# S4D convolution and SwiGLU on one core: skip term on TensorE, kernel stage in 64 by 64 pairs, loads in small paced pieces, and a new deal of the tasks

## The chip, the cores and the metric

The kernel runs on one core of one Trainium2 chip. The metric is device time in microseconds (us) of one execution. Three executions of the kernel before took 968.3, 971.08 and 966.05 us; the median is 968.3 us. The execution that the profiler recorded took 967.95 us, of which 966.0 us lie between its first and last instruction (the span).

## The reference, cut to what matters

The input u is 2048 tokens of 640 channels in float32. A six-fold modulation (shift, scale and gate, twice) comes from a small vector c through silu and one matrix. Then:

```
h = layernorm(x) * (1 + ca) + sa
K[d, l] = 2 Re sum_n C[d, n] exp(A[d, n] dt[d] l)          # 128 states, 2048 taps
y = irfft(rfft(h, 4096) * rfft(K, 4096))[:2048] + h * D_skip
x = x + ga * y
h = layernorm(x) * (1 + cb) + sb
x = x + gb * ((silu(h @ w1) * (h @ w3)) @ w2)              # 640 -> 1728 -> 640
```

The skip term h * D_skip is the same as adding D_skip[d] to the tap at lag 0 of the kernel K, and that is how both kernels make it.

## The kernel before, in words

**First stage (0 to about 350 us): the convolution.** The 640 channels are dealt in 5 blocks of 128 (b = 0 to 4). For each block the kernel K is generated in 8 chunks of 16 channels: GpSimd makes integer phases (`ph`) and products (`yy`, `xx`), ScalarE makes sines (`tr`), VectorE multiplies them on, and TensorE sums over the states into a bank `kps` (32 matmuls of 64 columns, on four tiles of 32 columns). ScalarE copies `kps` into `ks`, and VectorE adds D_skip to the one column in 64 that holds the tap at lag 0 (`skip`, L1342). A Fourier transform in two factors follows, by matmuls: the first factor turns `ks` (and the normalized input `xb`) into a bank `ps` (8 tasks for each block and each of the two, 8 matmuls of 128 columns in each task, L1400), which ScalarE or VectorE copy to `sp`; the second turns `sp` into the spectra `fh` (input) and `fk` (kernel). VectorE multiplies the spectra (`product`, `both`, L1446 and L1454, into `fp`), TensorE turns them back by one factor (`fz`), ScalarE or VectorE copy that to `zt`, and a DMA stores `zt` to the scratch `zd` in HBM.

**The tail (about 336 to 398 us).** When the last chunk of the last block is generated, its buffers are freed (`change`, L1113) and the second stage's buffers open in their place: the first 512 tokens (`low`), the matrix `wd` of the last transform, the first two tiles of the weights (`wr_0`, `wr_13`, `w2r`), and rows of `zd` for `iy`. `iy` (L551) is the last factor: it gives the convolution's output for the tokens, which VectorE adds to them. The 512 channels of the blocks 0 to 3 go first (two halves u = 0, 1), then the last 128 channels, read back when the last `zt` is stored ("the read-back"; its matmuls are L562). Between them stand 8 matmuls `awake`, whose result nobody reads. A layer norm of the tokens and four transposes of them follow.

**Second stage (398 us to the end): the feed-forward network.** Four token blocks of 512; the first two go through 14 tiles of the 1728 columns (`f-tiles`, in the order 0, 13, 1, 2, ...; tile 13 has 64 columns), each as three matmul products of a high and a low half of both operands (`gu`, L999 to L1001), then gate, split and `down` (`acc`, L1036). The last two blocks go together through `pair_up` and `pair_down`. Weights are loaded by `weights_load` (L667) one or two tiles ahead, split by ScalarE (`wh`, L693) and VectorE or GpSimd (`wl`).

**What sets the order.** In the first stage and the tail every engine's instructions stand in the order in which a table of task numbers, ORDER, deals the tasks (class Plan, L162; a letter behind a number picks the engine where a task can go to two). The class InOrder (L138) makes each engine keep that order; while its field `behind` is set, what is issued also waits for the last TensorE instruction that was issued before it. `held_back` (L1733) makes a DMA wait for the read-back's last matmul, once `hold` is set. SyncE's queue (SP) issues nearly all DMAs, in its own order; a DMA at its front that waits keeps those behind it.

## Time and profile before

| quantity | value |
|---|---|
| median of three executions | 968.3 us |
| profiled execution, its span | 967.95 us, 966.0 us |
| mean granted TensorE clock | 0.964 |
| TensorE matmuls busy | 856.0 us (89%) |
| VectorE busy | 713.6 us (74%) |
| ScalarE busy | 518.4 us (54%) |
| GpSimd busy | 336.2 us (35%) |
| moved by DMA | 113.20 MB, mean 117 GB/s |

A line of the groups reads: source line (L147 stands for all that goes through InOrder), engine, operation, output<-inputs, shape, count | busy us in all, mean ns of one | idle time of the engine ahead of them and what ended it. A line of the windows reads: stretch in us, its length, then for PE (matmuls), PEld (weight loads), DVE (VectorE), ACT (ScalarE) and POOL (GpSimd) the busy us and the number of instructions, then the granted clock, the busy share of the DMA engines and GB/s. A float32 matmul leaves two records, so 32 matmuls read x64.

### The profile page before, as it was taken

The numbers are of one execution on the slowest core, as the hardware profiler recorded it, in microseconds if no ns is written. First come the engines' busy times: TensorE is split into PE (matmuls) and PEld (weight loads), VectorE is DVE, ScalarE is ACT, GpSimd is POOL, SyncE is SP. The second block draws the span as 40 slices with busy tenths as digits, with TensorE's granted clock in tenths as the row PEclk, the third lists the DMA queues.
The fourth block names the chain that finished last, engine by engine and source line by source line (L and its number), as shares of the span: only waits on it lengthen the run. The fifth ranks groups of instructions, "written<-read, shape, count | busy, mean of one in ns | idle before, by whom it ended". The sixth has DMA issues, their size and how long they took to land.

```text
span 966.0 us, 20403 instructions
## 1 busy us (share of the span) xinstructions
PE 856.0 (89%) x8145; PEld 681.2 (71%) x8145; DVE 713.6 (74%) x1292; ACT 518.4 (54%) x874; POOL 336.2 (35%) x345
## 2 busy tenths in 40 slices
PE   2164867899999996899999999999999999999997
PEld 1033755787878772577787778888888888888875
DVE  7888899999999974565666486566468777765763
ACT  5889879979888840442343244344234444445331
POOL 2799898599999730100000000000113222300000
PEclk9597889999999997999999999999999999999999
DMA  9955426624040277875545263233031111123242
GB/s 245 253 172 209 106 61 168 162 70 111 25 111 25 69 224 230 200 202 150 158 121 137 82 157 103 82 85 106 28 82 55 55 55 55 42 82 92 86 150 82
DMA packets 124934, 113.20 MB, mean 117 GB/s; under 512 B 12328, under 2 KB 107048, under 8 KB 123432
## 3 DMA queue, kind: packets, MB, share of 16 engines
q1 hardware_dynamic: 124072, 110.99, 42.4%
q8 instruction: 64, 1.05, 0.5%
q10 hardware_dynamic: 768, 0.92, 0.4%
q14 instruction: 30, 0.25, 0.1%
HBM read 90.91 MB, written 20.97 MB: 116 GB/s over the span
## 4 chain that ended last, share of the span: by engine, by line
PE 57%; DVE 2%; DMA 2%; ACT 1%; issue 0%; SPq 0%; DVEq 0%; ACTq 0%
PE p L789 17%; PE acc L1036 16%; PE gu L999 7%; PE gu L1001 6%; PE gu L1000 6%; DMA wq<-in_w 1%; PE iy L562 1%; PE awake L147 1%; PE q L789 1%; PE tp L613 1%; PE fz L147 1%; DMA zd<-zt 0%; PE acc L147 0%; DVE w2l L988 0%; PE iy L147 0%; DVE wq L983 0%
## 5 line engine op out<-in xcount | busy, mean ns | idle before, releaser
L999 PE MATMUL gu<-xh,wh 128*128 128x512 f32 x270 | 106.0, 398 | 0.9 <-ACT xh L581 0.7
L1001 PE MATMUL gu<-xh,wl 128*128 128x512 f32 x270 | 105.4, 390 | 0.0
L1000 PE MATMUL gu<-xl,wh 128*128 128x512 f32 x270 | 105.2, 390 | 0.0
L789 PE MATMUL p<-x,wch 128*128 128x512 f32 x312 | 92.6, 390 | 0.0
L808 POOL TENSOR_TENSOR ws<-wp 128x256 f32<-128x256 f32 x13 | 9.6, 740 | 230.9 <-DVE x L582 116.0
L147 POOL TENSOR_TENSOR yy<-e,e 128x512 f32<-128x512 f32 x80 | 86.0, 1089 | 4.8 <-PE kps L147 3.6
L147 POOL TENSOR_TENSOR ph<-p,p 128x1024 int32<-128x1024 int32 x40 | 78.0, 1953 | 16.4 <-ACT tr L147 16.0
L147 DVE TENSOR_TENSOR yy<-yy,tr 128x512 f32<-128x512 f32 (+1 forms) x80 | 75.3, 946 | 1.6 <-POOL yy L147 1.2
L147 PE MATMUL kps<-yy,xx 128*32 128x64 f32 x2560 | 51.3, 235 | 23.2 <-DVE xx L147 12.9
L693 ACT ACTIVATE wh<-wr 128x640 fp32r<-128x640 f32 x51 | 34.9, 731 | 68.2 <-PE gu L1000 61.1
L147 PEld LDWEIGHTS kps<-yy,xx 128*32 128x32 f32 x2560 | 45.0, 117 | 34.0 <-issue 16.2
L789 PEld LDWEIGHTS p<-x,wch 128*128 128x128 f32 x312 | 58.3, 188 | 12.5 <-ACT s L824 0.4
L999 PEld LDWEIGHTS gu<-xh,wh 128*128 128x128 f32 x270 | 50.6, 188 | 16.8 <-issue 2.1
L1001 PEld LDWEIGHTS gu<-xh,wl 128*128 128x128 f32 x270 | 50.7, 188 | 11.3 <-DVE wl L702 0.4
L1000 PEld LDWEIGHTS gu<-xl,wh 128*128 128x128 f32 x270 | 50.7, 188 | 10.2 <-DVE xl L582 0.2
L789 PE MATMUL p<-x,wcl 128*128 128x512 f32 x156 | 57.0, 389 | 0.0
L147 ACT ACTIVATE tr<-ph,hpi 128x512 f32<-128x512 f32 x80 | 54.5, 689 | 3.0 <-DVE yy L147 2.1
L147 DVE TENSOR_TENSOR xx<-tr,xx 128x512 f32<-128x512 f32 x80 | 54.4, 682 | 1.7 <-ACT tr L147 1.5
L705 POOL MEMSET w2l<- 64x640 f32 x1 | 0.6, 632 | 157.0 <-PE acc L1036 157.0
L826 DVE TENSOR_TENSOR s<-p,s 128x512 f32<-128x512 f32 x52 | 34.8, 683 | 26.8 <-ACT s L824 22.8
L147 PE MATMUL ps<-wk,xb 128*64 128x128 f32 x640 | 46.8, 297 | 5.3 <-DVE hb L147 2.5
L1014 DVE TENSOR_TENSOR a<-a,gu 128x512 f32<-128x512 f32 x26 | 17.9, 687 | 45.5 <-PE gu L1001 45.4
(368 smaller groups left out, 2299.3 us busy)
## 6 DMA issues: line engine op xcount, KB each, us to landing
wr<-in_w SPq DMA_DIRECT2D x52, 320.0 KB, 3.6
zd<-zt SPq DMA_DIRECT2D x39, 256.0 KB, 2.7
w2r<-in_w SPq DMA_DIRECT2D x26, 320.0 KB, 3.0
wp<-in_w SPq DMA_DIRECT2D x26, 320.0 KB, 3.6
wq<-in_w SPq DMA_DIRECT2D x26, 320.0 KB, 3.2
low<-zd SPq DMA_DIRECT2D x48, 160.0 KB, 5.4
xs<-in_x SPq DMA_DIRECT2D x16, 320.0 KB, 9.8
hs<-hb SPq DMA_DIRECT2D x20, 256.0 KB, 2.7
```

The costliest lines, as they stand in the source:

```text
L147: self.prev = self.k.order(f(*a, **kw), self.prev)
L562: mm = nc.tensor.matmul(py[p][c:c + 32, :n], self.wd[r:r + 64, j0 + j + p, q // 2, c % 64:c % 64 + 32], z[q // 2][r:r + 64, j + p, o:o + n ...
L613: nc.tensor.transpose(pt[:, j * P:(j + 1) * P], xn[:, j, k * P:(k + 1) * P], self.ident)
L693: self.nc.scalar.activation(wh[:, i], raw[:, i], AF.Copy)
L789: nc.tensor.matmul(to, t[:, o], y[:, k], start=start and k == i == 0, stop=stop and (k, i) == (n - 1, 2), skip_group_check=True)
L808: G.tensor_tensor(s[0], a21, a22, op=ALU.add)
L826: add = lambda o, bk, s: V.tensor_tensor(o, bk, s, op=ALU.add)
L999: nc.tensor.matmul(pg, wh[:, k, :], xh[:, k, :], start=(k == 0), stop=False)
L1000: nc.tensor.matmul(pg, wh[:, k, :], xl[:, k, :], start=False, stop=False)
L1001: nc.tensor.matmul(pg, wl[:, k, :], xh[:, k, :], start=False, stop=(k == KT - 1))
L1014: nc.vector.tensor_mul(a, a, gu[1])
L1036: nc.tensor.matmul(acc[k], *two(a, w), start=(m == 0 and i == 0), stop=(m == 12 and i == 2))
```

## The change

1. **Skip term.** The 40 VectorE adds are gone. Ahead of each chunk's `kps` matmuls stand four matmuls `kps<-dsk,ident` of 4 columns, which write D_skip into the column for lag 0; the `kps` matmuls accumulate onto it. ScalarE's copy is then all that stands between `kps` and `ks`.
2. **Kernel stage.** For the blocks 1 to 4 the first factor of the kernel is 4 tasks of 32 matmuls of 64 columns on four tiles of 64 by 64 (`kernel_tasks`), where it was 8 tasks of 8 matmuls of 128 columns on two tiles. `ks` is two half tiles, so a half is free earlier. Each new task fills two banks, copied as before.
3. **Spectra products.** Two of the last block's eight products (APART = 2, 5) go to GpSimd, after a ScalarE copy of the kernel's spectrum into `sp`. A few table products move from VectorE to GpSimd.
4. **Loads.** The first tokens, the matrix `wd` (half as large now), the first two weight tiles and the rows of `zd` for `iy` are issued piece by piece, each behind the TensorE instruction issued last, dealt among the stores of `zt`; buffers of their own let the tokens and the weights be loaded before the generator's buffers are freed.
5. **Third f-tile.** For the first token block, `weights_load` wraps its DMAs in `held_back`: tile 1 and all later tiles wait for the read-back's last matmul, where tiles 1 and 2 were loaded ahead of it.
6. **ORDER** is a new table throughout.

```diff
         def product():
             kps = place()
+            b, c = d0 // P, d0 % P // C
+            last = kps.rearrange("p (e b) -> p e b", b=64)[:, :, 63]
+            for q in range(4):
+                s = slice(32 * q, 32 * q + 32)
+                nc.tensor.matmul(last[s], self.ident[:, s], self.dsk[:, b, 4 * c:4 * c + 4], start=True, stop=False,
+                                 tile_position=(0, 32 * q), skip_group_check=True)
...
-                                         start=(r == 0), stop=(r == 1), tile_position=(0, 32 * q))
+                                         start=False, stop=(r == 1), tile_position=(0, 32 * q), skip_group_check=True)
...
-        dma = (nc.gpsimd if ahead and POOLQ else nc.sync).dma_start
+        loads = []
+        dma = (lambda *a: loads.append(a)) if ahead else (lambda *a: self.held_back(nc.sync.dma_start(*a))) if b == 0 else nc.sync.dma_start
...
+        def paced(f):
             nc.sync.behind = nc.tensor.prev
-            self.load_x2(0)
-            nc.sync.dma_start(self.wd, self.t_wd)
+            f()
             nc.sync.behind = None
+
+        def load_tokens(i):
...
+            if i < 4:
+                paced(lambda: nc.sync.dma_start(self.x2[0][i * 32:(i + 1) * 32], self.xv[i, :, 0:4, :]))
+            else:
+                paced(lambda: nc.sync.dma_start(self.wd, self.t_wd))
...
+        def load_w(m, i):
+            if i == 0:
+                split[m] = self.weights_load(0, self.ORDER[m], None, True)
+            loads = split[m][0]
+            paced(lambda: [nc.sync.dma_start(*a) for a in (loads[2:] if i == 2 else loads[i:i + 1])])
+
+        def load_z(u, i):
+            paced(lambda: z.__setitem__(u, self.inverse_load(2560 if u else 0, 2 * u, 2, 0, cut, to=None if u else self.xb, part=i)))
...
-        def skip(c):
-            o = slice(4 * c, 4 * c + 4)
-            V.tensor_add(self.ks[b][:, o, 63], kps.pop(c).rearrange("p (e b) -> p e b", b=64)[:, :, 63], self.dsk[:, b, o])
...
+    def kernel_tasks(self, b):
...
+        def mm(i):
+            for h in range(2):
+                pk[i, h] = self.pbank(f"ps{b}1{i}{h}")
+            for e in range(8):
+                x = self.ks[b][i // 2][:, 8 * i % 16 + e, :]
+                for r in range(2):
+                    for h in range(2):
+                        g = slice(64 * h, 64 * h + 64)
+                        o = pk[i, h][r * 64:(r + 1) * 64].rearrange("p (v j i f) -> p i j v f", j=2, i=8, f=2)[:, e]
+                        nc.tensor.matmul(o, x[g], self.wk[g, r, g], start=True, stop=True, tile_position=(64 * h, 64 * r))
...
+            apart = b == NB - 1 and i in APART
...
+            on, took = ("POOL", (1.04, 1.04, 1.1)) if apart else ("DVE", (.61, .61, .67))
```

Where the order of instructions moves, two places matter. The first is SyncE's DMA queue in the tail. `zd<-zt` are the stores of the last block's transforms (`ztl` the same, from its own buffer), `low<-in_x` or `x_low<-in_x` the tokens, `in_t_wd` the matrix `wd`, `wr` and `w2r` raw weights of tile 0, 13, 1 and 2, `low<-zd` and `xb<-zd` 64x512 the rows for `iy`, `low<-zd` 64x2x128 the read-back. Before, from the tokens on:

```order
L147 DMA low<-in_x 32x2560 x4
L147 DMA low<-in_t_wd 128x2048
L147 DMA wr_0_4860<-in_w 128x5x128 x2
L147 DMA w2r_0_4863<-in_w 128x640
L147 DMA zd<-zt_4891 128x4x128
L147 DMA zd<-zt_4893 128x4x128
L147 DMA wr_13_4927<-in_w 128x5x64 x2
L147 DMA w2r_13_4930<-in_w 64x640 x2
L147 DMA low<-zd 64x512 x8
L677 DMA wr_1_5417<-in_w 128x5x128 x2
L147 DMA zd<-zt_5016 128x4x128
```

And now the queue's end, up to the first loads behind the read-back:

```order
L147 DMA low<-zd 64x512 x2
L147 DMA zd<-ztl 128x4x128
L147 DMA x_low<-in_t_wd 128x1024
L147 DMA low<-zd 64x512 x2
L147 DMA zd<-zt_5476 128x4x128
L147 DMA w2r_13_5280<-in_w 64x640 x2
L147 DMA low<-zd 64x512 x2
L569 DMA low<-zd 64x2x128 x4
L555 DMA x_5568<-in_x 32x2560 x4
L694 DMA wr_1_5789<-in_w 128x5x128 x2
L694 DMA w2r_1_5792<-in_w 128x640
L555 DMA x_5566<-in_x 32x2560 x4
```

The eight rows of `zd` in one go are now pairs between stores, `wd` has moved to the end of the tail, and tile 1's weights stand behind the read-back and behind four loads of tokens.

The second place is ScalarE's own list from the first FFN sigmoid on (`th`, `u`, `ah` are steps of the gate of tiles 0 and 13, `wh` the high halves of weights). It reads the same in both kernels; in the changed one:

```order
L1036 ACTIVATE th_0_5754<-gu_00_5701 128x512
L716 ACTIVATE wh_1_5794<-wr_1_5789 128x640 x2
L716 ACTIVATE wh_2_5884<-wr_2_5879 128x640 x2
L1042 ACTIVATE th_13_5778<-gu_130_5703 64x512
L1044 ACTIVATE u_5782<-gu_130_5703 64x512
L602 ACTIVATE ah_0_5756<-a_0_5755 128x512
```

So `ah_0`, which the first `down` reads, stands behind the high halves of tiles 1 and 2 in both.

More of the change, by code (lines that the diff above doesn't have):

```diff
@@ L622, in pair_x @@
     def pair_x(self, i, p=slice(None)):
[L624 removed]
+        return [self.px[i][h][:, p] for h in range(2)]
     def ln_pair(self, xh, xl, pool, ps):
@@ L711, in split @@
             return low(nc.vector)
-        return (high, low) if ahead else split
+        return (loads, high, low) if ahead else split
     ORDER = (0, 13) + tuple(range(1, 13))
@@ L1187, in between @@
                 xc = open_("xc")
-                self.px = [xc.tile([P, 2, 2 if i < 5 else 1, 512], F32R, name=f"x3_{i}") for i in range(6)]
+                x = self.xtile("pair", F32R)
+                part = lambda o, n: x[:, o:o + 512 * n].rearrange("p (k t) -> p k t", k=n)
+                tile_ = lambda i, h: xc.tile([P, 2 if i < 5 else 1, 512], F32R, name=f"x3_{i}{h}")
+                self.px = [[part(0, 2), part(1024, 2)], [part(2048, 2), tile_(1, 1)]] + [[tile_(i, h) for h in range(2)] for i in (2, 3, 4)] + [[part(3072, 1), tile_(5, 1)]]
             if (b, m) in ((0, 8), (1, 4)):
@@ L1368, in gen_tasks @@
                     give=[("tr", n + f"s{(0, 0, 1, 3, 4)[i]}")])
[L1369 removed]
+            add(n + "p", "PE", 1.1, lambda c=c: ch[c][4](), [n + f"m{i}" for i in range(5)] + (["dsk"] if b == 0 else []), t + 3,
                 take=[("kg", 1)], give=[("yy", n + "z0"), ("xx", n + "z2")])
[L1371 to L1372 removed]
+            add(n + "r", "ACT", .27, lambda c=c: rows(c), [n + "p"] + ([f"k{b - 1}.{i}.m" for i in (range(c // 4 * 2, c // 4 * 2 + 2) if b > 1 else range(c // 4 * 4, c // 4 * 4 + 4))] if b else ["exp0", "q0.t0", "q1.t0"]) + ([f"{g}.{c // 4 * 4}.r"] if c % 4 else []), t + 3, give=[("kg", n + "p")])
     def h_tasks(self, b):
```

279 lines of the change are left out of this document (158 added, 121 removed).

## The prediction

> **What bounds the kernel now.** I began with the chain of waits on the page, to see which engine sets the end, and went on to windows, because the share over the whole span mixes stages.
>
> ```profile
> PE 57%; DVE 2%; DMA 2%; ACT 1%; issue 0%; SPq 0%; DVEq 0%; ACTq 0%
> core 0: us, PE busy (x) PEld busy (x) DVE busy (x) ACT busy (x) POOL busy (x), PEclk, DMA share, GB/s
> 125.00:150.00 25.00, 16.56 (x340) 12.45 (x331) 24.66 (x48) 19.10 (x36) 23.79 (x25) 0.86 0.30 84
> 200.00:225.00 25.00, 24.79 (x474) 19.83 (x472) 24.71 (x47) 19.27 (x35) 21.73 (x23) 1.00 0.43 107
> 300.00:325.00 25.00, 24.80 (x538) 21.42 (x536) 24.38 (x45) 21.18 (x38) 24.27 (x21) 1.00 0.16 44
> ...
> 336.00:348.00 12.00, 10.96 (x213) 9.07 (x208) 6.47 (x14) 3.53 (x7) 0.00 (x0) 1.00 0.71 176
> 348.00:362.00 14.00, 13.26 (x166) 10.19 (x162) 11.96 (x26) 6.56 (x10) 8.27 (x6) 1.00 0.83 255
> 362.00:381.00 19.00, 10.58 (x65) 3.75 (x64) 8.56 (x22) 2.28 (x4) 0.00 (x0) 0.73 0.87 254
> 398.00:416.00 18.00, 17.81 (x76) 14.05 (x77) 11.03 (x16) 10.72 (x17) 2.64 (x2) 1.00 1.02 225
> ```
>
> Three stages with three limits. From 125 to 150 us VectorE is full (24.66 of 25) and TensorE is not (16.56). From 200 to 325 both are full, so there work taken from VectorE alone frees nothing. In the tail no engine is full: from 362 to 381 TensorE is busy 10.58 of 19 us, VectorE 8.56, and the DMA engines 0.87 at 254 GB/s. From 398 on TensorE is full (17.81 of 18). So the kernel can gain ahead of 398 us, and lose anywhere. The chain through the tail:
>
> ```profile
> 362.99 4.15 DMA zd<-zt
> ...
> 367.22 0.60 ACT zt L147
> ...
> 380.04 1.28 DVE low L147 x2
> ...
> 381.36 7.13 PE awake L147 x16
> 388.49 0.56 PE iy L562 x22
> ...
> 396.70 0.78 ACT v L616
> ...
> 416.07 3.40 PE acc L1036 x15
> ```
>
> A store of `zt` that lands late holds a buffer, ScalarE waits for it, and `iy` and the last `fz` come behind. SyncE's list says why the store was late:
>
> ```profile
> 355.78 5.91 SPq L147 DMA_DIRECT2D low<-zd  x8
> 361.79 1.10 SPq L677 DMA_DIRECT2D wr<-in_w  x2
> 362.99 0.47 SPq L147 DMA_DIRECT2D zd<-zt  x1
> ```
>
> It stood behind eight reads of `zd` (5.91 us to issue) and tile 1's weights. I mark G = 336.6, the start of the last `kps` chunk (its row is below), and H = 388.49 + 0.56 = 389.05, the end of the read-back's matmuls. The tail takes 52.4 us from G to H. From 336 to 381 it moves, by the three windows, 12 x 0.176 + 14 x 0.255 + 19 x 0.254 = 10.5 MB. At 0.25 MB/us that is 42 us: a stage bound by its transfers and their order.
>
> **The change part by part: up to G.**
>
> ```profile
> L147 PEld LDWEIGHTS kps<-yy,xx 128*32 128x32 f32 x2560 | 45.0, 117 | 34.0 <-issue 16.2 <-POOL p L147 7.9 <-POOL step L147 4.2
> L147 DVE TENSOR_TENSOR ks<-kps,dsk 128x4 f32<-128x4 f32 x40 | 6.1, 158 | 5.4 <-PE kps L147 3.4 <-ACT ks L147 2.0
> L147 DVE TENSOR_TENSOR fk<-fk,hq 128x512 f32<-128x512 f32 x40 | 27.5, 690 | 0.0
> L147 DVE TENSOR_TENSOR fp<-fp,fk 128x256 f32<-128x256 f32 x80 | 29.6, 412 | 0.1
> L147 POOL TENSOR_TENSOR yy<-e,e 128x512 f32<-128x512 f32 x80 | 86.0, 1089 | 4.8 <-PE kps L147 3.6 <-DVE hn L147 0.6 <-POOL ph L147 0.6
> 336.63 1.17 PE L147 MATMUL kps<-yy,xx 128*32 128x64 f32 x64
> ...
> 343.52 1.99 PE L147 MATMUL fz<-fp,wz 64*128 64x512 f32 x8
> 345.44 2.84 PE L147 MATMUL ps<-wk,ks 128*64 128x128 f32 x48
> ```
>
> VectorE loses the 40 skip adds, 6.1 us, and with the copies that now fall to ScalarE and the table products that fall to GpSimd about 10 us up to G (counted in both orders, priced by the rows of their kinds), of which some 8 lie in block 1, in the stretch that VectorE bounds. Its 5.4 us of waiting ahead of these adds go as well. ScalarE takes about 5 us more; by the windows it has 4 to 6 us in 25 to spare.
>
> TensorE gains on `ps`: an old task takes 2.84 / 3 = 0.95 us. A pair task has the 64 records of 64 columns on four tiles that a `kps` task has, so I take 1.17 us from that row, for two old ones (1.9). That gives back 4 x 0.73 = 2.9 us a block. If only two of the four tiles ran at once it would be 2.3 us, a loss of 1.6 us a block. TensorE pays for the skip matmuls, which have no row yet. Lower bound: 8 records at the pitch of `kps` (1.17 / 64 = 0.018 us), 0.15 us a chunk; upper bound: 8 weight loads of 117 ns one after the other, 0.94 us. I take 0.2, near the lower end, since they are tiled by 32 columns as `kps` is and none depends on another. A block pays 8 x 0.2 = 1.6 us and saves 2.9.
>
> The Trainium skill, TensorEngine Tiling (Array Packing), section Performance Considerations (Instruction Overhead), puts some 60 cycles on each matmul, however few its columns; the 18 ns pitch here is shorter than that would be at full clock. The same page, Tiling Modes (Key Properties), says that a change of tiling mode drains the array, which speaks against a third mode in this stage. The queue of TensorE shows the last `kps` up to 336.63 + 1.17 = 337.80 with the next work close behind it, so no drain stands out; if each of some 32 new changes cost a weight load of 117 ns, it would take back 3.7 us.
>
> As both engines are full from 200 on, the 1.3 us a block saved on TensorE and the little that VectorE loses there come only as far as the new deal lets them. Block 1's relief, up to 8 us, passes only in part, since GpSimd is busy 23.79 of 25 us there. **G: 5 us earlier (10 earlier to 3 later).**
>
> **From G to H.** Gone from the tail: most of the tokens and of tiles 0 and 13 go before G, `wd` is half, tiles 1 and 2 (6 x 0.33 = 1.97 MB) go behind H. That leaves about 6.4 MB, 26 us at 0.25, and no more than two reads of `zd` ahead of a store. So transfers no longer fill it. What does, counted from G: the last two pair tasks and their copies, 4.2 us. Six products on VectorE (2 x 0.69 + 2 x 0.41 = 2.2 us each, 13.2), with a few copies, to 19.4. The two on GpSimd lie beside these, at about 4 us each by the 1089 ns of its `yy` product. The last `fz` (1.99 us) and `zt` (0.60), to 22.4. Then the queue: `wd` now stands behind the `ztl` store and the last rows of `zd` behind tile 13's second matrix, so I put the second `iy` at 30 (29.5 to 30.5); its adds (1.28) end at 31.8; `awake`, which waits for the bank that these adds free, takes 7.13, to 38.9. The last read-back also waits, on ScalarE, behind tile 13's high halves; I have it landed at 33.5 to 35.5, under `awake`'s cover. With 0.56 us of matmuls H is at G + 39.4, against 52.4: **13 us earlier (21 earlier, if the queue's order costs nothing and only compute stays; 5 earlier, if it stalls the stores as before).**
>
> **From H on.** One swap on ScalarE puts a second `v` (0.78 us) ahead of the first `xh`: +0.8 us. Then the held weights:
>
> ```profile
> 407.77 2.62 ACT L693 ACTIVATE wh<-wr 128x640 fp32r<-128x640 f32 x4
> ...
> 411.52 0.63 ACT L581 ACTIVATE ah<-a 128x512 fp32r<-128x512 f32 x1
> ...
> 422.58 1.60 ACT L693 ACTIVATE wh<-wr 128x640 fp32r<-128x640 f32 x2 [6.92 <-DMA wr<-in_w]
> ```
>
> Before, `wh` of tiles 1 and 2 ran at 407.77, H + 18.7, on data that had long landed. Now ahead of tile 2 in the queue lie tokens (1.31 MB), tile 1 (0.98), tokens (1.31) and rows of `zd` (1.31); with itself (0.66) that is 5.57 MB, at the 0.225 MB/us of the window from 398 24.8 us, and with 1.8 us that I allow for landing H + 26.6. Tile 1 (2.3 MB by then) lands at H + 12, in time. ScalarE waits at the second `wh` with `ah_0` behind it. From that `wh`'s start (407.77 + 1.3) to `ah_0`'s end (412.15) were 3.1 us, then comes VectorE's low half, 0.7: the first `down` starts at H + 30.4, against 416.07 - 389.05 + 0.8 = H + 27.8. TensorE works in order, so it stands for 2.6 us. Tile 3 lands some 8 us later after H than before. ScalarE had already waited 6.92 us for it without TensorE feeling it, so most is hidden; I add 1.4 us for the rest. **+4 us (1 to 8).** From tile 4 on nothing changes.
>
> **Sum**, against the profiled execution's 967.95 us: -5 - 13 + 0.8 + 4 = -13.2, hence 954.8; the median is 0.35 us above that execution, so I forecast **955 us**. Its own range, if the four terms err apart from each other, is 948 to 961.
>
> **The rivals.** *Partial gain.* The tail's pieces wait in the order of the queue, and the last read-back behind tile 13's matrix: the tail gives 6, the hold costs 6, G gains 3: 968.3 - 6 + 6 + 0.8 - 3 = 966. For it: one store in the tail stood 7 us behind other issues, and a piece that waits for TensorE now holds the stores behind it. Against: 4 MB fewer pass there. *Larger gain.* G comes 9 us earlier, the tail gives 18, because the stores and the last reads land under the products, and the hold costs 2: 968.3 - 9 - 18 + 0.8 + 2 = 944. For it: VectorE is full to 325 us and loses 10 us of work. Against: TensorE is full beside it from 200 on. *Slower.* The skip matmuls run one after the other, at 0.94 us a chunk, 0.74 more than I take; over the 24 chunks of the blocks 2 to 4, where TensorE is full, 18 us: 973. From 0.35 us more a chunk (8.4 us) the gain falls under 5 us. For it: a weight load of 117 ns stands with each record. Against: 64 such records end in 1.17 us. *It doesn't do what it says*: the hold stands in SyncE's list as a wait and the skip term in TensorE's, so I give that nothing.
>
> **How the numbers follow.** Chances: forecast 0.46, partial 0.20, larger 0.22, slower 0.12. Less than 0.5% (4.8 us) can't be told from no change here. Faster: the forecast but for 0.02, the larger gain, 0.09 of the partial: 0.75. Same: 0.02, 0.09 of the partial and 0.03 of the slower: 0.14. Slower: 0.02 of the partial and 0.09: 0.11. The range, 941 to 968, takes in the larger gain with 3 us below it and the partial with 2 above; most of the slower case stays out.
>
> **What would show it.** In the changed profile a chunk of `kps` with its skip matmuls takes 1.4 us (right) or 2 (the slower rival), and a pair task 1.2. G stands near 331. From G to H are 40 us, with `awake` right ahead of the read-back and the DMA share under 0.7. ScalarE waits 3 to 7 us for `wr` at a `wh` about 25 us behind H, and the first `down` comes some 30 behind it. A store of `zt` held by a paced load, or a gap of several us on TensorE at the second `iy`, would show that I read the queue wrong. From the fifth f-tile on the two traces should run at one distance, the total difference; if not, the forecast is wrong in a place that I did not price.

## The result: slower by 1.3%, and the profile after

Four executions of the changed kernel took 978.34 to 982.17 us, median 981.02, beside 966.05 to 971.08 us, median 967.48, of the kernel before. The ratio is 1.013 with a 95% interval of 1.0095 to 1.0166: slower by some 13.5 us, where I had forecast 955 us, 13 us faster. The profiled execution has a span of 980.4 us against 966.0. The distance between the two traces, along marks that both have, in us:

| mark | before | after | after later by | added since the mark above |
|---|---|---|---|---|
| last `kps` chunk starts (G) | 336.63 | 348.31 | 11.7 | +11.7 |
| read-back's last matmul ends (H) | 389.80 | 394.46 | 4.7 | -7.0 |
| first `gu` | 398.05 | 404.93 | 6.9 | +2.2 |
| first `down` | 415.91 | 422.83 | 6.9 | 0 |
| `gu` behind the third f-tile, to `pair_down` | | | 11.5 | +4.6 |
| end of the span | 966.0 | 980.4 | 14.4 | +2.9 |

(In the prediction H was 389.05: the read-back's last eight records, to 389.80, were left out there.) By blocks (their ends are in the table of the experiments), 1.8 of the 11.7 us arise in block 0, 2.9 in block 1, 7.0 in block 2 and none behind it. The last 2.9 us arise in `pair_down`: TensorE stands 3.1 us there in five places for `w2l`, which VectorE makes, against 1.1 in one place before. Ten of the twelve kernels below grow by 2.2 to 3.8 us there too, so this can't be put down to one part of the change.

The windows of the first stage, at the stretches that the prediction showed and at two more, columns as there. The kernel before at the two new stretches:

```profile
110.00:125.00 15.00, 12.57 (x282) 11.59 (x285) 14.64 (x26) 13.27 (x25) 12.30 (x15) 1.00 0.39 107
235.00:250.00 15.00, 14.19 (x302) 12.22 (x300) 14.98 (x27) 14.68 (x24) 14.08 (x12) 1.00 0.21 60
```

The changed kernel:

```profile
110.00:125.00 15.00, 8.84 (x144) 8.18 (x146) 7.22 (x14) 9.30 (x15) 4.93 (x8) 0.66 0.31 89
125.00:150.00 25.00, 15.59 (x332) 14.12 (x328) 22.65 (x40) 21.32 (x41) 21.63 (x24) 0.93 0.37 101
200.00:225.00 25.00, 22.84 (x586) 18.35 (x575) 23.64 (x39) 23.28 (x44) 22.93 (x24) 1.00 0.47 119
235.00:250.00 15.00, 11.99 (x194) 8.22 (x193) 11.62 (x22) 11.58 (x18) 9.31 (x10) 0.77 0.21 57
300.00:325.00 25.00, 23.21 (x724) 20.59 (x725) 22.84 (x38) 21.92 (x39) 23.55 (x25) 1.00 0.13 30
```

VectorE was full in every one of these stretches before. Now it stands 7.8 of 15 us from 110 on and 3.4 of 15 from 235 on, and the other engines stand in the same stretches, so no engine is the limit there. The granted clock is down as well, 0.66 and 0.77. I call these two stretches holes in the deal: places where every engine waits for another. The first, on the time line of VectorE, ScalarE and TensorE (start, us, then the instruction; in brackets the idle time ahead of it and what ended it):

```profile
107.20 1.76 DVE L147 TENSOR_SCALAR hn<-xq,rs_y_h,rs_n_h 128x128 f32<-128x128 f32 x4 [2.27 <-ACT sp L147]
...
111.20 0.68 DVE L147 COPY sp<-ps 128x512 f32<-128x512 f32 x1
...
111.96 1.94 ACT L147 ACTIVATE hn<-xq,rs_n_h,rs_y_h 128x128 f32<-128x128 f32 x4 [4.80 <-issue]
...
115.28 2.00 PE L147 MATMUL ps<-wk,xb 128*64 128x128 f32 x16 [6.59 <-DVE sp L147]
```

`hn`, the normalized input of block 1, goes into the same four PSUM banks (where TensorE's results land) as `ps`. VectorE's `hn` waits for a bank that ScalarE's `sp` copy frees. ScalarE's `hn` then starts at 111.96, as VectorE's copy of 111.20 ends (111.88). The profile names no releaser for this wait ("issue"); from the times and the table I read that the copy frees its bank, and the table deals the copy behind VectorE's own `hn` and three more instructions. The run on the two holes, below, bears this out. The second hole, on TensorE:

```profile
239.50 1.09 PE L147 MATMUL fz<-fp,wz 64*128 64x512 f32 x2 [1.52 <-DVE fp L147]
242.09 3.31 PE L147 MATMUL fz<-fp,wz 64*128 64x512 f32 x6 [1.49 <-ACT hq L147]
245.32 1.99 PE L147 MATMUL ps<-wk,ks 64*64 64x64 f32 x64
```

The inverse `fz` waits first for a product (`fp`) that VectorE makes last of three, then for ScalarE's `hq`; the matmuls that follow take nearly twice their time (`ps` took 1.16 at 343.80, below).

The small prices held:

```profile
343.80 1.16 PE L147 MATMUL ps<-wk,ks 64*64 64x64 f32 x64
...
348.22 0.24 PE L147 MATMUL kps<-dsk,ident 128*32 128x4 f32 x8
348.31 1.15 PE L147 MATMUL kps<-yy,xx 128*32 128x64 f32 x64
...
351.48 1.75 PE L147 MATMUL ps<-wk,ks 64*64 64x64 f32 x104 [1.51 <-issue]
```

A pair task is 1.16 us (forecast 1.17), and the skip matmuls move the product by 348.31 - 348.22 = 0.09 us (forecast 0.2). But TensorE also stands with nothing named that it waits for, as in the last line. From 80 to 362 us there are nine such stops, 9.2 us in all, five of them in pair tasks; the kernel before has one, of 0.77 us.

In the tail, VectorE, at the first of the last block's products and at the first behind a product of GpSimd:

```profile
355.66 0.69 DVE L147 TENSOR_TENSOR fp<-fk,hq 128x512 f32<-128x512 f32 x1 [1.66 <-PE fk L147]
...
367.53 0.69 DVE L147 TENSOR_TENSOR fp<-fk,hq 128x512 f32<-128x512 f32 x1 [1.90 <-POOL fp L147]
```

TensorE:

```profile
371.62 1.99 PE L147 MATMUL fz<-fp,wz 64*128 64x512 f32 x8 [1.37 <-DVE fp L147]
381.48 2.07 PE L147 MATMUL iy<-xb,x_low 64*32 64x512 f32 x16 [7.87 <-DMA x_low<-in_t_wd]
383.15 2.98 PE L147 MATMUL iy<-low,x_low 64*32 64x512 f32 x16
386.06 7.13 PE L147 MATMUL awake<-x_low,ident 128*128 128x512 f32 x16
393.12 0.64 PE L583 MATMUL iy<-low,x_low 64*32 64x128 f32 x24
```

and SyncE's queue ahead of it:

```profile
373.64 1.09 SPq L147 DMA_DIRECT2D low<-zd  x2
374.82 0.54 SPq L147 DMA_DIRECT2D zd<-ztl  x1
375.41 0.50 SPq L147 DMA_DIRECT2D x_low<-in_t_wd  x1
```

The matrix `wd` stands behind the store `ztl`, which is ready only when the last `fz` (to 373.61) is. The chain of waits gives its flight as "375.41 5.93 DMA": until 381.34 no `iy` can run, neither the first nor the second.

In the second stage, ScalarE's waits for held weights, and TensorE behind the second of them:

```profile
418.64 0.74 ACT L716 ACTIVATE wh<-wr 128x640 fp32r<-128x640 f32 x1 [2.61 <-DMA wr<-in_w]
...
433.16 1.51 ACT L716 ACTIVATE wh<-wr 128x640 fp32r<-128x640 f32 x2 [8.11 <-DMA wr<-in_w]
```

```profile
436.59 0.50 PE L1023 MATMUL gu<-xh,wh 128*128 128x512 f32 x1 [2.73 <-DVE x L588]
...
438.42 0.63 PE L1025 MATMUL gu<-xh,wl 128*128 128x512 f32 x1
```

The first wait (2.61) reaches nobody: the first `down` keeps its distance. The second (8.11) does: the chain of waits runs from `wr` over this `wh` and VectorE's low half to the add (`x`) that releases TensorE. TensorE stands 2.73 us, and the `gu` that follow take up to 0.63 us until about 440 us, where others take 0.39.

### The profile page after: what moved, and what is told of

The parts are those of the page before. It is cut to its first block, busy times and chain, and to the rows that moved or that the text cites. A ratio compares the mean times of both kernels' runs of the same rounds, so it can differ in the third digit from the quotient of the medians.

```text
span 980.4 us, 22049 instructions
## 1 busy us (share of the span) xinstructions
PE 862.8 (88%) x8977; PEld 682.6 (70%) x8977; DVE 701.7 (72%) x1233; ACT 520.7 (53%) x883; POOL 346.4 (35%) x357
## 4 chain that ended last, share of the span: by engine, by line
PE 66%; DMA 7%; ACT 7%; DVE 5%; issue 3%; SPq 1%; DVEq 0%; ACTq 0%
PE p L813 16%; PE acc L1060 14%; PE gu L1023 6%; PE gu L1025 6%; PE gu L1024 6%; PE ps L147 5%; PE fz L147 3%; PE kps L147 3%; PE fk L147 2%; DMA wq<-in_w 2%; DMA low<-zd 2%; ACT tr L147 2%; PE fh L147 2%; DMA wr<-in_w 1%; DVE fp L147 1%
## 5 line engine op out<-in xcount | busy, mean ns | idle before, releaser
L1024 PE MATMUL gu<-xl,wh 128*128 128x512 f32 x270 | 105.7, 392 | 0.0
L813 PE MATMUL p<-x,wch 128*128 128x512 f32 x208 | 68.3, 389 | 0.0
L147 PE MATMUL kps<-yy,xx 128*32 128x64 f32 x2560 | 48.8, 229 | 16.8 <-DVE xx L147 14.5
L147 POOL TENSOR_TENSOR yy<-e,e 128x512 f32<-128x512 f32 x48 | 52.0, 1095 | 6.4 <-PE kps L147 2.8
L147 PEld LDWEIGHTS ps<-wk,xb 128*64 128x64 f32 x640 | 43.9, 219 | 13.0 <-DVE sp L147 6.8
L147 PE MATMUL fz<-fp,wz 64*128 64x512 f32 x160 | 46.6, 650 | 6.5 <-DVE fp L147 4.0
```

Source lines behind the costliest of these rows:

```text
L147: self.prev = self.k.order(f(*a, **kw), self.prev)
L813: nc.tensor.matmul(to, t[:, o], y[:, k], start=start and k == i == 0, stop=stop and (k, i) == (n - 1, 2), skip_group_check=True)
L1024: nc.tensor.matmul(pg, wh[:, k, :], xl[:, k, :], start=False, stop=False)
```

## The experiments

All are compared with executions of the kernel before on the same chip; ratios have 95% intervals. The changed kernel itself is at 1.013. In the table, G and H are as above, and the five columns are the ends of each block's last `kps` chunk, from TensorE's time line.

| kernel | median us, ratio | block 0, 1, 2, 3, 4 | G to H |
|---|---|---|---|
| before | | 105.7, 176.3, 238.8, 291.0, 337.8 | 53.2 |
| after | 981.02, 1.013 (1.0095 to 1.0166) | 107.5, 181.0, 250.5, 301.2, 349.5 | 46.1 |
| hold undone | 973.87, 1.0059 (1.0029 to 1.0088) | 105.4, 178.8, 246.8, 297.7, 345.9 | 45.9 |
| tail's loads in another order | 972.43, 1.0063 (1.0034 to 1.0092) | 104.4, 178.1, 247.2, 297.4, 346.2 | 39.7 |
| both | 969.41, 1.0011 (0.9996 to 1.0026) | 105.5, 178.6, 246.4, 296.6, 344.7 | 43.4 |
| old deal | 984.03, 1.0165 (1.0139 to 1.019) | 106.4, 176.3, 240.6, 298.1, 345.2 | 53.2 |
| pair shape undone | 981.71, 1.0138 (1.0115 to 1.0162) | 103.9, 177.7, 249.1, 300.6, 349.9 | 46.7 |
| both, no skip term | 971.13, 1.0043 (1.0021 to 1.0065) | 108.6, 180.2, 249.0, 299.2, 348.6 | 43.6 |
| before + skip on TensorE | 969.52, 1.0022 (1.0003 to 1.0042) | 104.4, 174.5, 236.3, 289.1, 335.0 | 53.9 |
| both + two holes mended | 964.58, 0.9959 (0.9941 to 0.9977) | 105.8, 175.2, 242.7, 294.0, 342.4 | 43.5 |
| both + first hole | 966.61, 1.0001 (0.9981 to 1.002) | 104.3, 174.4, 244.2, 294.9, 343.7 | 43.5 |
| both + second hole | 969.58, 1.0025 (1.0005 to 1.0045) | 104.0, 177.7, 243.3, 294.4, 343.6 | 43.4 |
| both + fillers | 974.21, 1.007 (1.0047 to 1.0093) | 105.3, 178.7, 252.5, 304.0, 354.0 | 46.0 |
| two holes mended, weights behind the read back | 963.9, 0.9965 (0.9944 to 0.9986) | 104.6, 173.0, 236.9, 288.9, 337.9 | 43.6 |

One caution: kernels whose first stage is dealt alike differ by up to 5 us in block 4's end in their one profiled execution (after, hold undone, pair shape undone, tail's loads, both, no skip: 344.7 to 349.9). The medians carry the verdicts, the traces the places. Each ratio is to the kernel before on the same chip; the medians of two rows may come from different chips.

### The hold

```diff
-        dma = (lambda *a: loads.append(a)) if ahead else (lambda *a: self.held_back(nc.sync.dma_start(*a))) if b == 0 else nc.sync.dma_start
+        dma = (lambda *a: loads.append(a)) if ahead else nc.sync.dma_start
```

> The changed kernel (981.0 us) with one part undone: the weights of the third and later f-tiles no longer wait for the read-back, all else as changed. Theory (the hold costs the time between the first gu and the fifth f-tile, where the distance to the kernel before grows from 6.9 to 11.5 us): 976 to 979 us, the distance stays near 7 us behind the fifth f-tile, and ScalarE's waits for wr of 2.6 and 8.1 us are gone; up to 2.6 us of it is given back in the tail, where 0.66 MB of weights enter the queue again ahead of the last stores. Rival (the weights only trade places with other loads): 980 to 982 us, the same distance.

973.87 us, 7.1 less than the changed kernel (by the ratios, 0.007 x 968 = 6.9), and a little under what the theory allowed. In its trace the distance to the kernel before is 1.55 us at the first `gu` and 1.6 at the start of `pair_up`: the 4.6 us are gone. ScalarE still waits for the weights, though I had expected that to go,

```profile
422.55 1.59 ACT L716 ACTIVATE wh<-wr 128x640 fp32r<-128x640 f32 x2 [5.32 <-DMA wr<-in_w]
```

but 5.32 us is covered, as the kernel before covered 6.92, and 8.11 was not.

### The order of the tail's loads

In the table of tasks only: `wd` (fx4) goes right behind the last tokens (fx3), and the pieces of `iz1` and of tile 13's weights ahead of the stores, so that nothing but stores is left behind the last `fz`.

> The changed kernel with seven load tasks dealt earlier in the tail: the matrix wd behind the last piece of the tokens, the rows of zd for the second iy and tile 13's weights behind the rows for the first, all ahead of the last stores. Theory (the tail lost its gain to wd, which stands behind the ztl store: TensorE waited 7.9 us for it at the first iy): the wait goes, the read-back's matmuls end 5 to 8 us earlier against the last chunk, 973 to 977 us. Rival (another wait takes its place: the stores come later behind these loads, or the last rows read back land no earlier): 979 to 983 us.

972.43 us, 8.6 less than the changed kernel, 6.5 by the ratios. The time line of TensorE, and one line of ScalarE's:

```profile
368.38 1.99 PE L147 MATMUL fz<-fp,wz 64*128 64x512 f32 x8 [1.38 <-DVE fp L147]
370.29 1.06 PE L147 MATMUL iy<-xb,x_low 64*32 64x512 f32 x8
373.62 0.60 ACT L147 ACTIVATE zt<-fz 128x512 f32<-128x512 f32 x1 [5.93 <-DMA zd<-zt]
374.27 0.63 PE L147 MATMUL iy<-xb,x_low 64*32 64x512 f32 x4 [2.92 <-ACT zt L147]
...
376.20 7.13 PE L147 MATMUL awake<-x_low,ident 128*128 128x512 f32 x16
383.26 0.70 PE L583 MATMUL iy<-low,x_low 64*32 64x128 f32 x24
```

The first half of the first `iy` follows the last `fz` with no wait, where it stood 7.87 us, and G to H is 39.7 us. The rival is there as well: the last stores now stand behind the loads, ScalarE waits 5.93 us for one of them before it can copy a `zt`, and the rest of the `iy` waits 2.92 us for that copy. That 39.7 is near the 39.4 of my forecast for the change itself is chance: the items differ (see why the prediction was wrong).

### Both

> The changed kernel with two edits at once: the tail's loads issued in the order that already took the tail from 46.1 to 39.7 us, and the third f-tile's weights no longer tied to the read back. Theory (the two losses lie one behind the other on the path and add): 6.5 + 7 us less than the changed kernel, so 967 to 970 us, the last chunk's product at 344 to 349 us as in every kernel of this deal, first gate matmuls at 392 to 396, and no growth of the distance to the kernel before behind the third f-tile. Rival (the weights, free to be issued early, share the DMA engines with the read back and take back what the new order won): 972 to 975 us.

969.41 us, ratio 1.0011: no difference from the kernel before that can be told. The two losses add, as the theory had it, within 2 us. G to H is 43.4 us, not 39.7, and the read-back waits four times for its rows, of which the first and the third are

```profile
382.26 1.03 PE L583 MATMUL iy<-low,x_low 64*32 64x128 f32 x8 [0.73 <-DMA low<-zd]
...
384.87 0.64 PE L583 MATMUL iy<-low,x_low 64*32 64x128 f32 x4 [0.65 <-DMA low<-zd]
```

SyncE issued the third tile's weights at 370.08, ahead of the last stores. That fits the rival, at a small price, but the last run below doesn't confirm that these weights cost the 3.7 us.

### The old deal under the new code, and the pair shape undone

The old table of tasks, its names mapped to the new tasks and repaired where a dependency forbade it:

> The changed kernel with its tasks in the order of the kernel before (pair tasks where the second of the two old tasks stood, the pieces of the loads where the whole loads stood). Theory A (the new deal of the tasks costs the first stage its 11.7 us): the last chunk of kps starts at 330 to 337 us instead of 348.3, 964 to 972 us. Theory B (the operations cost it: pair tasks that need two banks at once, skip matmuls, tables in other buffers): the last chunk still starts at 345 us or later, 978 to 985 us.

The matmuls of a pair task in their old shape, the same deal and the same two banks:

```diff
-            for e in range(8):
-                x = self.ks[b][i // 2][:, 8 * i % 16 + e, :]
-                for r in range(2):
-                    for h in range(2):
-                        g = slice(64 * h, 64 * h + 64)
...
-                        nc.tensor.matmul(o, x[g], self.wk[g, r, g], start=True, stop=True, tile_position=(64 * h, 64 * r))
+            for h in range(2):
+                for e in range(4):
+                    x = self.ks[b][i // 2][:, 8 * i % 16 + 4 * h + e, :]
+                    for r in range(2):
...
+                        nc.tensor.matmul(o, x, self.wk[:, r, :], start=True, stop=True, tile_position=(0, 64 * r))
...
```

> The changed kernel, same tasks, same order, same banks; only the matmuls in a pair task are the old ones (16 of 128 columns on two tiles for 32 of 64 columns on four). If the 64 by 64 shape is worth what its row says (1.1 us for 1.9 us, 16 tasks) and TensorE bounds these stretches: 986 to 994 us, last chunk 5 to 13 us later. If TensorE waits for other engines there: 979 to 984 us, last chunk within 3 us of 348.3. If the changes of tiling mode cost more than the shape saves: below 979 us.

The old deal gave 984.03 us, with block 4's end at 345.2: the time that theory B had, and the theory that the new deal alone had made G late fell in this form. But the places differ. With the old deal the blocks 1 and 2 end near those of the kernel before (176.3 and 240.6 us against 176.3 and 238.8), and the loss comes in block 3 (57.5 us from block 2's end to its own, against 52.2). TensorE stands 2.14 us there with nothing named (until 278.25), and behind its work VectorE stands 3.43 us for `fk` (until 282.29); whether that is all of it is open. With the new deal the loss is there by block 2 (246 to 250 us). Of theory B's operations, the pair shape (this section) and the skip matmuls (the next) cost nothing; pair tasks that need two banks at once, and tables in other buffers, had no run of their own.

The pair shape is worth nothing here: 981.71 us without it against 981.02, though a pair task takes 1.16 us and two old ones 1.9. TensorE waits for other engines in this stage (23.21 of 25 us busy from 300 on, above). Most of the unnamed stops go with the shape: without it there are two from 80 to 362 us, 2.4 us, where the changed kernel has nine, 9.2 us. As the time is the same either way, no run here shows that they cost anything.

### The skip term: left out, and alone

The skip matmuls, four to a chunk, 160 in all (320 records; the expectation counts records), left out of the kernel with both edits (its output lacks the skip term):

```diff
...
-                nc.tensor.matmul(last[s], self.ident[:, s], self.dsk[:, b, 4 * c:4 * c + 4], start=True, stop=False,
-                                 tile_position=(0, 32 * q), skip_group_check=True)
...
-                                         start=False, stop=(r == 1), tile_position=(0, 32 * q), skip_group_check=True)
+                                         start=(r == 0), stop=(r == 1), tile_position=(0, 32 * q))
```

> The kernel of the run with both edits, without the 320 matmuls that put the skip term into the product (the skip term is left out of the output). Theory (TensorE waits for the other engines in the generation, so 40 times some 0.1 us of its time is worth nothing): the last product ends within 2 us of the other kernels of this deal (344 to 349 us), the time within 2 us of theirs. Rival (the longer stream of TensorE instructions is what made the generation late): the last product at 337 to 341 us and a time 5 to 8 us lower.

And the other way round, the kernel before with the skip matmuls put in and its 40 adds and their tasks taken out:

> The kernel before, its deal, loads and tail untouched, with one edit of the change alone: the skip term by eight TensorE matmuls in each chunk, and the 40 small DVE additions gone. Theory (the skip term is not what made the generation late): last product at 335 to 339 us (336.6 to 337.3 in the kernel before), time 965 to 970 us. Rival (it is: the matmuls stand in front of each product): last product at 341 to 346 us, time 972 to 977 us.

Without them 971.13 us, against 969.41 with them: they cost nothing. Alone, in the kernel before, 969.52 us, ratio 1.0022, so they bring nothing either. That speaks to the step on VectorE's relief: block 1 lasts from 104.4 to 174.5, 70.1 us, against 105.7 to 176.3, 70.6. (Block 4 ends 2.8 us earlier than before in this trace, no more than such traces differ.) VectorE without the adds, from 125 to 150 us:

```profile
125.00:150.00 25.00, 16.28 (x334) 11.94 (x330) 24.59 (x45) 19.53 (x38) 24.09 (x27) 0.86 0.38 102
```

It is as full as before (24.66), and so is GpSimd (24.09). In this run the distance to the kernel before also grows at the end, in `pair_down`, from -2.0 to +0.2 us. That stage's code is untouched here, so the change need not be what cost the changed kernel 2.9 us there.

### The two holes

The table of tasks of the kernel with both edits, with two places mended. First hole: two `sp` copies on VectorE (of `hh0.0` and `hh0.7`) go ahead of the `hn` work (`h1.1.n`, `h1.0.x`). Second: the product `w1.5` goes ahead of `w1.6` and `w1.7` on TensorE and VectorE, the inverse `z1.2` that needs it ahead of `w2.6.f`, and one pair task (`k2.0.m`) two places back.

> The kernel of the run with both edits, with tasks moved at two places of its deal: behind the first block two DVE copies out of PSUM go ahead of the two normalisations that held their banks (ACT stood 4.80 us there), and in the third block one spectrum product and its inverse are dealt ahead of two others (TensorE stood 1.5 + 1.5 us there and then ran at half clock). Theory (the deal's own two holes are what made the generation late): block 1 starts some 4 us earlier, the last chunk of the third block ends at 238 to 243 us instead of 246 to 250, the last product at 337 to 342 us, the time 959 to 965 us. Rival (VectorE and ScalarE, about 70% busy, bind over the whole stage, and an engine that gets out of a hole early waits at the next): last product 343 us or later, the time within 2 us of the kernel with both edits.

> The kernel with both edits of the tail and the weights (969.4 us, last product at 344 us), with only the first of the two places mended: the two DVE copies dealt ahead of the normalisations behind block 0. Theory (the two places are two losses one behind the other, and their shares of the 4.8 us add): block 1 starts 3 to 4 us earlier, last product 1.5 to 3 us earlier (341 to 342.5), time 966 to 968. Rival (what is won at block 1 is waited away by block 4, and the second place carries it all): last product at 344 us or later, time 968.5 to 970.

> The same base with only the second place mended: in block 2 the spectrum product that an inverse waits for is dealt ahead of two others. Theory (shares add): block 2 ends at 242 to 244 us instead of 246, last product 341 to 343, time 966 to 968. Rival (this place carries it all): time 964 to 965.5, last product at 339 to 341; or nothing, 968.5 to 970, if the first does.

Both places together: 964.58 us, ratio 0.9959 (0.9941 to 0.9977), 4.8 us less than with the holes and faster than the kernel before. At the two places:

```profile
105.49 1.95 ACT L147 ACTIVATE hn<-xq,rs_n_h,rs_y_h 128x128 f32<-128x128 f32 x4
...
110.29 2.00 PE L147 MATMUL ps<-wk,xb 128*64 128x128 f32 x16 [3.24 <-DVE sp L147]
...
231.10 1.99 PE L147 MATMUL fz<-fp,wz 64*128 64x512 f32 x8 [0.28 <-DVE zt L147]
...
239.06 1.68 PE L147 MATMUL ps<-wk,ks 64*64 64x64 f32 x64 [1.49 <-ACT zt L147]
```

and the window behind the second (the third figure from the end of a row is the granted clock):

```profile
240.00:245.00 5.00, 5.00 (x122) 4.12 (x118) 4.19 (x7) 3.33 (x7) 2.42 (x4) 0.71 0.21 57
```

At the first place ScalarE's wait of 4.80 us is gone and TensorE's 6.59 us are 3.24. Four kernels with this hole and the same first stage (after, hold undone, tail's loads, both) take 73.1 to 73.7 us for block 1; with it mended block 1 takes 69.4 us, with it alone mended 70.1 and in the last run 68.4, against 70.6 before. The second place is mended only in part. The inverse's waits of 1.52 and 1.49 are 0.28, but behind it TensorE now stands 0.96 us for `hq` and 1.49 for `zt`, and the granted clock is 0.71. Block 2 takes 67.8 to 69.8 us where the hole is as it was, 67.5 and 65.6 in the two kernels here that mend it and 63.9 in the last run, against 62.5 before.

One place alone brings less than can be told: 966.61 and 969.58 us, ratios 1.0001 and 1.0025 against 1.0011. So the two shares do not simply add, and neither form of the expectation holds. Single traces, with the differences that they have, do not show where the gain of one place goes. Behind block 2 little happens: from its end to block 4's all these kernels take 98 to 101 us, and the kernel before 99.0.

### The clock at the second hole

In the kernel with both edits, matmuls that nobody reads (into the half of the `kps` bank that stands empty) ahead of the inverse `z1.2` and within it, for its two waits:

```diff
+            warm = (b, j) == (1, 2)
+            for i in range(12 if warm else 0):
+                nc.tensor.matmul(self.kg[:, 1], self.ident, self.wk.rearrange("p r n -> p (r n)"), start=True, stop=True)
             for r in range(2):
                 for f in range(2):
+                    for i in range(11 if warm and (r, f) == (0, 1) else 0):
+                        nc.tensor.matmul(self.kg[:, 1], self.ident, self.wk.rearrange("p r n -> p (r n)"), start=True, stop=True)
```

> The kernel with both edits, and 23 matmuls that nobody reads in front of and within the inverse of block 2 for which TensorE stood 1.5 and 1.5 us: they fill the waits, and the order of the work is unchanged. Theory (the granted clock falls because TensorE stands, and the fall, 0.56 to 0.77 in 235 to 245 us, lengthens what follows: 3.78 us for six inverse matmuls that take 1.98 us elsewhere): clock at 0.95 or more through 235 to 250 us, the last chunk of block 2 ends 2 to 4 us earlier (242 to 244 us), time 0 to 3 us lower (966.5 to 969.5). Rival (the clock falls for another reason, or the filler only stands in the way): clock below 0.8 in one of these windows, block 2 ends at 246 us or later, time 969 to 971.

The windows of the kernel with both edits, without the fillers (granted clock 0.77 and 0.55):

```profile
235.00:240.00 5.00, 2.86 (x6) 1.13 (x7) 3.26 (x6) 4.77 (x8) 3.88 (x6) 0.77 0.00 0
240.00:245.00 5.00, 5.00 (x83) 3.27 (x81) 2.89 (x5) 2.23 (x3) 1.59 (x2) 0.55 0.39 107
```

and with them, clock 1.00 in both:

```profile
235.00:240.00 5.00, 5.00 (x35) 4.36 (x32) 4.83 (x10) 4.97 (x9) 4.49 (x6) 1.00 0.01 3
240.00:245.00 5.00, 5.00 (x21) 3.50 (x21) 0.19 (x1) 1.55 (x3) 2.74 (x2) 1.00 0.02 3
```

TensorE with them:

```profile
235.82 5.45 PE L147 MATMUL kps<-wk,ident 128*128 128x256 f32 x24
241.20 1.12 PE L147 MATMUL fz<-fp,wz 64*128 64x512 f32 x2
242.25 5.02 PE L147 MATMUL kps<-wk,ident 128*128 128x256 f32 x22
247.20 1.98 PE L147 MATMUL fz<-fp,wz 64*128 64x512 f32 x6
249.11 1.16 PE L147 MATMUL ps<-wk,ks 64*64 64x64 f32 x64
```

At this place the clock falls because TensorE stands: kept busy, it keeps 1.00. The Trainium skill, TensorE: Matmul & The Clock Gate, section HAM oscillation — how this bites in real kernels, warns of idle gaps over some 3.4 us; here two of 1.5 us with 1.1 us of work between them were enough. The length of the waits doesn't settle it, though: behind waits of 0.96 and 1.49 us the clock was 0.71 in the kernel with both holes mended, and behind 0.93 and 1.49 at the same place it was 1.00 in the last run, where the pair task took its 1.16 us:

```profile
234.56 1.16 PE L147 MATMUL ps<-wk,ks 64*64 64x64 f32 x64 [1.49 <-ACT zt L147]
```

What decides is not shown here. The price of the fall at the place of the fillers: six records of the inverse 3.78 us instead of 1.98, the pair task 1.98 instead of 1.16, 2.6 us for these two. But my fillers were more than three times too long (5.45 + 5.02 = 10.5 us for waits of 3.0), so they stood in the way, and the kernel was slower, 974.21 us. The part of the expectation on the clock held, the one on the time did not; fillers of the right length were not tried.

### The weights right behind the read back

To the kernel with both holes mended, an order without a wait: the third and later tiles' weights are issued on SyncE's queue behind the read back's last load.

```diff
-        dma = (lambda *a: loads.append(a)) if ahead else nc.sync.dma_start
+        dma = (lambda *a: loads.append(a)) if ahead else (lambda *a: self.then(nc.sync.dma_start(*a))) if b == 0 else nc.sync.dma_start
...
+    def then(self, i):
+
+        return self.order(i, self.read)
```

> The kernel with both places mended (964.6 us), with the third and later f-tiles' weights issued right behind the read back's four SP loads instead of anywhere before them: neither waiting for the read back to be used (as in the changed kernel) nor ahead of it (as in the run with both edits, where the tail took 43.4 us instead of 39.7). Theory (the 3.7 us that the tail lost there are the weights' transfers ahead of the read back): last product to the last read-back matmul 39.5 to 41.5 us, no growth of the distance to the kernel before at the third f-tile, time 960.5 to 963. Rival (issued behind the read back, the weights come too late for the third f-tile, as in the changed kernel): tail as in the theory, but gate matmuls some 2 to 5 us later behind the second f-tile, time 963.5 to 967.

963.9 us, ratio 0.9965 (0.9944 to 0.9986): the same as without it (0.9959), and faster than the kernel before. The forecast of 960.5 to 963 us failed, and G to H did not come down:

```profile
370.18 8.79 PE L147 MATMUL awake<-x_low,ident 128*128 128x512 f32 x16 [2.16 <-DVE x_low L147]
378.90 0.65 PE L586 MATMUL iy<-low,x_low 64*32 64x128 f32 x24
```

The read-back doesn't wait for its rows (24 records in one go), but `awake` starts after a wait of 2.16 us for VectorE's adds, and takes 8.79 us instead of 7.13. Neither comes from this order: in the kernel with both holes mended, where the weights are issued ahead of the last stores, the read-back runs in one go too, `awake` waits 2.75 us and takes 8.83, and G to H is 43.5. So the run doesn't show what the place of these weights costs. Why `awake` waits there, and not in the kernel with both edits or with the tail's loads alone, is open.

## Why the prediction was wrong

**Up to G: "5 us earlier (10 earlier to 3 later)"; it came 11.7 us later in the trace.** This is the step that failed, by 17 us. I counted the work that VectorE loses and let a part of it come out as time, on windows where VectorE was full. Both halves of that were wrong. Of the 10 us of work, the 6.1 of the adds, taken away alone, bring nothing (ratio 1.0022, block 1 shorter by 0.5 us); from 125 to 150 us GpSimd is nearly full beside VectorE (23.79 of 25 us), for which I had allowed only in part. The copies and table products that moved had no run of their own. And a new deal does not keep the engines as full as the old one: I had read what each engine runs in the new table, not when a PSUM bank is freed for the next task that needs one. The two holes are visible in the table (a copy that frees a bank stands on one engine behind a task that waits for a bank itself; an inverse stands behind the one product that is made last), and mending them gives 4.8 us. The first accounts for block 1. In block 2, where 7.0 of the 11.7 us arose, 1.4 to 5.0 us are left with the second mended, and TensorE's new waits behind that place (0.96 and 1.49 us) lie there. Block 4 then ends at 342.4 and 337.9 us in two kernels with the same first stage (337.8 before). That the deal alone is the cause is not shown: the old deal under the new code lost time too (block 4's end at 345.2), in block 3.

**The small prices up to G** held: the skip matmuls at 0.09 us (I had 0.2; the slower rival, 0.94, is refuted), the pair task at 1.16. "The 1.3 us a block saved on TensorE" was worth nothing: with the pair shape undone the time is the same. The stops in the middle of pair tasks had no price in my sum.

**From G to H: "13 us earlier (21 to 5)"; 7.0.** Inside its range, with the right mechanism, but H came 6.7 us later than G + 39.4, by two items of the sum that were too small. First, my sum ended the last `fz` at G + 21.4 (19.4 + 1.99; with `zt` that is 22.0, not 22.4, but nothing hangs on it); it ended at 25.3. I had let the products start behind the pair tasks, at 4.2. The first starts at 355.66, G + 7.4: a stop of 1.51 us in the pair tasks and the matmuls of the second factor (`fh`, `fk`) stand ahead of it. And the products on GpSimd, which I had laid beside VectorE's, made VectorE stand 1.90 us. Second, I saw that `wd` stands behind the `ztl` store and let only the second `iy` wait for it. The wait itself was about what I had put between the last `fz` and that `iy` (8.6 us; 7.87), but the first `iy` needs the same matrix, so both halves of `iy` stood behind it (4.6 us). With `wd` issued earlier the last `fz` still ends at G + 25.3; that G to H is 39.7 there, near my 39.4, is chance, as a wait for a store (2.92 us on TensorE) takes the place of the one for `wd`.

**From H on: 0.8 us for the swap; 2.2.** The transposes ran at a granted clock of 0.58 (4.04 us, from 399.63 on) where they had 1.00 (2.41 us), which I had not priced. Nor could I have from the wait ahead of them: it is 2.40 us here, 2.33 before, and 2.40 with the hold undone, where the clock was 1.00 again.

**The hold: "+4 us (1 to 8)"; 4.6.** The size is right, the place is not. I let the first `down` wait 2.6 us and gave tile 3 1.4. The first `down` did not move, and tile 3 took it all: ScalarE's wait for it went from 6.92 us, which TensorE does not feel, to 8.11 us, which it does. (In two other kernels with the hold, old deal and pair shape undone, ScalarE's first wait was longer, 4.52 and 3.51 us, and the first `down` did move, by 1.5 and 1.0 us.) Undone, the hold gives back 6.9 us by the ratios, whose intervals allow 2.4 to 11.

**The rivals.** The partial gain had the right mechanisms (a piece that stands behind a store, the hold's price) and the wrong sign, because its G was still earlier. My slower rival was on an operation that costs nothing; a new deal that makes engines wait for each other I did not have as a rival, though the range of G was the place for it. Nor does "948 to 961" follow from the ranges of the four terms: added as squares, they give about 945 to 967. The result lies outside both.

**What I said would show it.** A chunk with its skip matmuls took 1.24 us, a pair task 1.16, the DMA share from G to H was 0.57, ScalarE's wait for `wr` 24 us behind H was 2.6 us (I had 3 to 7), and the first `down` came 28.4 us behind H (I had 30). G was not near 331, and G to H not 40. The gap of several us on TensorE came, at the first `iy` and not the second: I had read the queue wrong. The distance is one, 11.5 us, from the fifth f-tile up to `pair_down`, and then grows by 2.9: by my own sign, a place that I did not price.

## What to carry to other kernels

A new order of the same work, dealt over engines that share a few buffers, is a change of its own, and its sign need not be that of the work it saves: look for the place where every engine stands at once, and ask there which instruction frees the buffer and what stands ahead of it on its engine. A saving on one engine counts only where the windows show the others with room. When a load is moved back in a queue, list everything that reads it, not only the step that one has in mind.

## What the runs showed of the hardware that I had not expected

Two gaps of 1.5 us on TensorE, 1.1 us of work apart, cost another 2.6 us through the granted clock, 0.55 to 0.77 in the windows behind them; kept busy with useless matmuls, the clock stayed at 1.00. Gaps as long elsewhere cost it or did not: 0.71 and 1.00 behind 1.49 us at one place in two kernels, 0.58 and 1.00 behind 2.40 us ahead of the transposes. 46 records of 128x256 f32 fillers took 10.5 us, 0.23 us each. TensorE also stands in the middle of runs of small matmuls with nothing named that it waits for: 9.2 us in nine stops in the changed kernel (1.51 us in a pair task until 351.48, on the chain that ended last), 7.9 us in ten in the last run, 2.4 us in two with the pair shape undone, 0.8 us in one before. No run here shows why, or that the time would be shorter without them.
